# Chunk attention and a swish MLP on one core: the transposition of one more unit goes to the transfers, and list positions move in blocks 1, 2 and 6 to 8

## The chip, the cores and the metric

The kernel runs on one core of a Trainium2 chip. The time is the device time of one execution in microseconds (us); several executions are taken and their median is quoted. The engines are named as the profile names them: PE is TensorE (matmuls), PEld its weight loads, DVE VectorE, ACT ScalarE, POOL GpSimd and SP SyncE. In this kernel POOL and SP issue transfers only, POOL the loads of inputs, SP the stores of outputs and the transposing transfers.

## What is computed

The inputs are q, k and v of 8 batches x 8 heads x 576 positions x 64, and an MLP with `w_in` (512 x 2048), `w_out` (2048 x 512) and a `beta` for each of the 2048 hidden columns.

```python
# attention inside chunks of 64 positions, for every batch and head
scores = scale * np.matmul(q_c, k_c.transpose(0, 1, 2, 4, 3))
attn = softmax(scores)                      # over the 64 keys of the chunk
x = np.matmul(attn, v_c) -> (4608, 512)     # tokens x (heads * 64)
# MLP with swish-beta
h = x @ w_in
g = h * (1.0 / (1.0 + np.exp(-beta * h)))
out = g @ w_out                             # 4608 x 512, float32
```

## The kernel before

**Units and blocks.** Tokens are worked in 18 units of 256 (four chunks, all eight heads) and nine blocks of 512 tokens, so block j holds units 2j and 2j+1. All matmul operands are float16, the sums float32.

**A unit of attention.** `load_qk` and `load_v` bring q, k and v in from POOL's queue. `emit_T` turns q and k around (head dimension onto the partitions). Up to unit XU−1 this is done by two VectorE transposes (L164) out of 256 KB loads (L112); from unit XU on by two transposing transfers on SP's queue (L159), and then each load is made of two halves of 128 KB with another layout (L106). XU is 9 before. After each `emit_T(u)` the loads of units up to u+4 are issued, as far as they have not been; four buffers for q and four for k set when POOL may issue them, three each for the turned tiles. `emit_sc` makes the scores in one of two forms: 64 matmuls of K=32 (L232) up to XU−1, 32 matmuls of K=64 (L219) from XU on; then ACT takes the exponential (L241, L225). `emit_pv` multiplies by v, with a column of constants that gives the denominators (L270; L256 from unit 8). `emit_norm` divides on VectorE, one half of the unit at a time (L307 and L313 up to unit 7; other lines from unit 8, where WV begins). The normalised half x is turned either on PE with a copy on ACT (`emit_xt_pe`, L329, units 0 to 5) or by a transposing transfer on SP (`emit_xt_dma`, L348, issued right after each norm, units 6 on). The result, `xt`, is what the first matmul of the MLP reads.

**The first matmul of the MLP.** `emit_m(j, m)` makes 128 of the 2048 hidden columns of block j: four matmuls of 128x512 into a PSUM tile `hps` (L372), tanh on ACT (L384) and the gate on VectorE (L360), which writes `gt`. From block QB = 6 on only the columns m = 0 to 3 go this way, with a silu on ACT (L381) and a scale `mg` on VectorE (L356). The other three groups of columns (i = 1, 2, 3) are formed by seven products of 256-wide sub-blocks in place of eight: `emit_q(j, i, s)`, in four steps s, into two PSUM tiles `qx` and `qz` (L484), with copies by ACT (L503) and adds by VectorE (L506) into `hq`. `emit_q_silu(j, i, part)` then runs two silus on ACT (L513) for part 2, 1 or 0, each on a quarter of `hq`, and `emit_q_scale` (L527) writes `gt`.

**The second matmul.** It also takes seven products for eight, in the order 1, 2, 6, 5, 7, 3, 4, each in two halves of eight 128x256 matmuls (L585). `emit_wt` (L427) and `emit_sum` (L436) form the sums of `w_out` and of `gt` that some products use, on VectorE. The accumulators of a block are two PSUM tiles, `ya` for products 1, 6, 7, 4 and `yb` for 2, 5, 3 (for block 1 they come from the four `ps_p` buffers and are called `acc`; while those are in use, in block 2, two buffers are left for `hps` and for the other tiles of that pool). An accumulator is read out after products 1, 6, 5 and 4 by an ACT copy (L602) and after 2, 7 and 3 by a VectorE add (L605), and the store goes out on SP (L539).

**What sets the order.** Nothing is reordered by a scheduler: instructions stand on each engine in the order in which the program emits them. For blocks j = 1 to 8 that order is a list. Each item has a position between 0 and about 1 in the block and a priority for equal positions; the list is sorted and emitted (lines 738 to 851). In block j the list holds the first matmul of block j (`m`, or the `LANE` of m and q items), the second matmul of block j−1 (`prod`, `sum`), and attention of the units of later blocks (`sc`, `pv`, `norm`, `T`). Block 2 also has attention of unit 5, and units 6 and 7, which block 3 reads; block 3 has units 8 to 10. `T 8`, `T 9` and `T 10` are in block 2's list. In blocks 6 to 8 a q item with step 2 brings two silu items (parts 2 and 1) and a scale item; their positions come from c, e and f, which are the lane's positions at that item, one item on and two items on.

Of the kernel before, what the change touches and what calls it, by code (L numbers as in the profile page):

```python
# [8 lines left out]
FP32 = mybir.dt.float32  # L9
# [6 lines left out]
def kernel(  # L16
# [16 lines left out]
    KFF = DFF // 128  # L33
# [21 lines left out]
    ps_y, qs_p, osl_p = [], [], []  # L55
# [20 lines left out]

    blocks = [(u, 2) for u in range(0, NU, 2)]
    NB = len(blocks)
    XU = 9
    WV = 8  # L80
    QB = 6
    unit_block = {}
# [15 lines left out]
    def load_qk(u):  # L98
        for src, dst, nm in ((q, q_t, "qu"), (k, k_t, "ku")):
            t = qk_p.tile([128, H, 2, D], FP16, tag=nm, name=nm)  # L100
            if u >= XU:
                dst[u] = t
# [46 lines left out]
    qT = {}  # L149
    kT = {}  # L150

    def emit_T(u, which=("kT", "qT")):
        for nm in which:
# [3 lines left out]
            dst[u] = t  # L157
            if u >= XU:
                nc.sync.dma_start_transpose(  # L159
# [50 lines left out]
    def emit_sc(u, split=False):  # L210
        qt, kt = qT.pop(u), kT.pop(u)
        sc = ps_s[0].tile([128, 2, H, CH], FP32, tag="s", name="sc")
        if u >= XU:
            qx, kx = (t.rearrange("p h s e -> p (h s e)").rearrange("p (j c t) -> p j c t", j=H, c=2)
# [29 lines left out]
    def emit_pv(u, halves=(0, 1)):  # L244
        et = et_t[u]
        if u >= WV:
# [3 lines left out]
            for n in (7, 0, 1, 2, 3, 4, 5, 6):  # L250
                for r in range(2):
# [3 lines left out]
                    for c in range(2):  # L255
                        nc.tensor.matmul(  # L256
                            out=o[64 * c:64 * c + 64],
                            lhsT=(et[64 * r:64 * r + 64, g % 2, 4 * s + 2 * c + g // 2, :] if u >= XU
                                  else et[64 * r:64 * r + 64, s, 4 * c + g, :]),
# [292 lines left out]
    def emit_prod(j, p, t):  # L552
        last = j == NB - 1
        if p == 1 and t == 0:
            if j == 1:
                a = [ps_p[0].tile([128, 512], FP32, tag="p", name="acc") for _ in range(2)]
            else:
                a = [ps_y[0].tile([128, 512], FP32, tag=n, name=n) for n in (("yb", "ya") if last else ("ya", "yb"))]
            if last:
                a = [[ps_p[0].tile([128, 512], FP32, tag="p", name="acc") for _ in range(2)], a]  # L560
            acc_t[j] = a
        g = gt_t[j]
        acc = acc_t[j][0 if p in (1, 6, 7, 4) else 1]
        acc, dst = (acc[t][:, 0:256],) * 2 if last else (acc, acc[:, 256 * t:256 * t + 256])
        c0 = t * 128
        for kk in range(8):
            lhsT = {
                1: lambda: g[:, kk, c0:c0 + 128],
                2: lambda: g[:, 8 + kk, c0:c0 + 128],
                3: lambda: sm[3][:, kk, c0:c0 + 128],  # L570
                4: lambda: g[:, 8 + kk, 256 + c0:256 + c0 + 128],
                5: lambda: sm[0][:, kk, c0:c0 + 128],
                6: lambda: sm[1][:, kk, c0:c0 + 128],
                7: lambda: sm[2][:, kk, c0:c0 + 128],
            }[p]()
            rhs = {
                1: lambda: w_at(0, kk, 0),
                2: lambda: w_at(1, kk, 0),
                3: lambda: w_at(1, kk, 1),
                4: lambda: wt[3][:, kk, :],  # L580
                5: lambda: wt[0][:, kk, :],
                6: lambda: wt[1][:, kk, :],
                7: lambda: wt[2][:, kk, :],
            }[p]()
            nc.tensor.matmul(  # L585
                out=dst,
                lhsT=lhsT,
                rhs=rhs,
                start=(p in (1, 2, 5) and kk == 0 and (t == 0 or last)),
                stop=(kk == 7 and (t == 1 or last)),  # L590
                skip_group_check=True,
            )
        if t == 0 and not last:
            return
        flush_stores()
        r, c, how = {1: (0, 0, "copy"), 2: (0, 0, "add"), 6: (0, 1, "copy"), 5: (1, 1, "copy"),
                     7: (1, 1, "add"), 3: (0, 1, "add"), 4: (1, 0, "copy")}[p]
        key = (j, r, c, t if last else None)
        if how == "copy":
            o = osl_p[0].tile([128, 256], FP32, name="osl") if last else osb_p.tile([128, DM], FP32, tag="osb", name="osb")  # L600
            oq_t[key] = o
            nc.scalar.copy(out=o, in_=acc)  # L602
        else:
            o = oq_t[key]
            nc.vector.tensor_tensor(out=o, in0=acc, in1=o, op=ALU.add)  # L605
        if p in (2, 7, 3, 4):
            late.append(key)
# [6 lines left out]
    with tc.manual_schedule():  # L614
# [104 lines left out]
        def att_items(u, a0, w):  # L719
            it = [(a0, 2, ("sc", u)), (a0 + 0.36 * w, 3, ("pv", u)), (a0 + 0.361 * w, 3, ("norm", u, 0)),  # L720
                  (a0 + (0.42 if u >= WV else 0.50) * w, 3, ("norm", u, 1))]
            if u >= WV:
                it.append((a0 + (0.45 * w if u == 9 else 0.005), 3, ("T", u + 3)))
            return it

        ATT = {2: ((6, 0.36, 0.27), (7, 0.60, 0.27)),
# [11 lines left out]
        for j in range(1, NB):  # L738
# [6 lines left out]
            items = []  # L745
            if j == 1:
                items += [(0.04 * m, 0, ("h", m)) for m in range(8)]
                items += [(0.32 + 0.0850 * (m - 8), 0, ("m", m)) for m in range(8, KFF)]
                items += [(0.30, 3, ("T", 4)), (0.52, 2, ("sc", 4)), (0.70, 2, ("pv", 4)), (0.71, 3, ("norm", 4, 0)),
                          (0.80, 3, ("norm", 4, 1)), (0.56, 3, ("Th", 5, "kT")), (0.63, 3, ("Th", 5, "qT"))]  # L750
                items += [(c, 3, ("wt", i)) for i, c in ((1, 0.47),)]
            else:
                m0 = {2: 0.36, 4: 0.09}.get(j, 0.02)
                if j < QB:
                    items += [(m0 + (1 - m0) * m / KFF, 0, ("m", m)) for m in range(KFF)]
                else:
                    lane = LANE[2 if j == QB else j == NB - 1]
                    cost = [1 if it[0] == "q" and it[2] == 3 else 2 for it in lane]
                    for n, it in enumerate(lane):
                        c, e, f = (0.98 * sum(cost[:n + d]) / sum(cost) for d in (0, 1, 2))  # L760
                        items.append((c, 0, it))
                        if it[0] == "m":
                            items.append((c + 0.04, 3, ("mg", it[1])))
                        elif it[0] == "last":
                            pass
                        elif it[2] == 2:
                            if j == NB - 1 and it[1] == 3:
                                f = e
                            items += [(f - 0.002, 2, ("qs", it[1], 2)), (f - 0.001, 2, ("qs", it[1], 1)),
                                      (f + 0.03, 3, ("qt", it[1], 0))]  # L770
                        elif it[2] == 3:
                            items += [(c + 0.001, 2, ("qs", it[1], 0)), (c + 0.04, 3, ("qt", it[1], 1))]
                    if j == QB:
                        items.append((0.01, 6, ("open",)))
                        items += [(0.011+0.001*n, 6, ("tx", QB, n)) for n in range(4)]
                    if j + 1 < NB:
                        items += [(0.70 + 0.06 * n, 5, ("tx", j + 1, n)) for n in range(4)]
                for i, p in enumerate((1, 2, 6, 5, 7, 3, 4)):
                    for t in range(2):
                        w = 1.06 if j == NB - 1 else 0.98  # L780
                        items.append(((0.002 if j >= QB else 0) + w * (2 * i + t) / 14, 1, ("prod", p, t)))
                if j == NB - 1:
                    for i, c in ((2, 0.72), (0, 0.80), (1, 0.86)):
                        items.append((c, 4, ("pre", i)))
                for i in range(4):
                    s0 = (0.01, 0.08, 0.25, 0.33)[i] if j == 2 else 0.005 + 0.07 * i
                    if j >= QB:
                        s0 = (0.08, 0.15, 0.33, 0.48)[i] if j == QB else (0.003, 0.10, 0.33, 0.48)[i]
                    items.append((s0, 4, ("sum", i)))
                if j == 2:  # L790
                    items += [(c, 3, ("wt", i)) for i, c in ((2, 0.36), (3, 0.55))]
                    items += [(0.03, 0, ("sc", 5)), (0.06, 2, ("xp", 4, 0)), (0.09, 2, ("xp", 4, 1)),
                              (0.17, 2, ("pv", 5)), (0.18, 3, ("norm", 5, 0)), (0.19, 3, ("norm", 5, 1)),
                              (0.24, 3, ("T", 6)), (0.53, 3, ("T", 7)), (0.60, 3, ("T", 8)), (0.61, 3, ("T", 9)), (0.80, 3, ("T", 10)),
                              (0.30, 2, ("xp", 5, 0)), (0.32, 2, ("xp", 5, 1))]
                for jw, i, c, d in ((3, 2, 0.10, 0.22), (4, 1, 0.21, 0.22), (4, 3, 0.10, 0.22)):
                    if jw == j:
                        items += [(c + d * n, 5, ("ws", i, n)) for n in range(4)]
                for u, a0, w in ATT.get(j, ()):
                    items += att_items(u, a0, w)  # L800
# [90 lines left out]
```

## Time and profile before

| Quantity | us |
|---|---|
| Median of three runs | 276.55 |
| Lowest and highest | 276.26, 276.83 |
| The profiled execution's own time | 276.39 |
| Its span in the profile | 274.6 |
| PE busy in the span | 266.6 |
| DVE, ACT, POOL busy | 210.0, 166.8, 95.2 |

The span is the part of the execution that the hardware profiler covers; the execution's own time is 1.8 us longer. PE is busy for 97% of the span, from about 17 us on nearly without a break. The granted TensorE clock of the profile is 1.00 in every stretch asked for. The page also lists how busy the DMA engines are: nines (90% and more) in the first 25 of 40 slices, up to about 172 us, and mostly one to three tenths from about 190 us.

The timeline view gives for each group of instructions its start, the busy time from the first start to the last end, the engine, the line, the operation with its tiles, the form, the count, and in brackets the idle time of that engine before the group with what ended it. Matmuls are pipelined, so neighbouring groups of PE overlap a little. `L372` is line 372 of the kernel printed above.

In these terms block 2 runs from about 63 us to 96.5, block 3 begins at 96.49, the blocks with q groups lie after 183 us, and the last block begins near 233.

### The profile page before, as it was taken

What the parts mean: (1) busy time and instruction counts of PE and PEld (TensorE: products, weight loads), DVE (VectorE), ACT (ScalarE), POOL (GpSimd) and SP (SyncE); (2) the same over time, 40 slices, a digit from 0 to 9 for tenths busy, and PEclk for the clock granted to TensorE, in tenths of its full rate; (3) what the DMA queues carried; (4) which work ended last, traced back from release to release, by engine and by line L of the source; (5) the groups of instructions that cost most, each with busy time, mean ns of one, the idle gap of its engine ahead of it and who ended that gap; (6) DMA issues with size and microseconds to landing.
All of it is one profiled execution on the core that took longest, in us unless ns stands there. A gap on an engine that the chain in (4) does not pass through costs nothing.

```text
span 274.6 us, 7824 instructions
## 1 busy us (share of the span) xinstructions
PE 266.6 (97%) x3237; PEld 184.8 (67%) x3237; DVE 210.0 (76%) x394; ACT 166.8 (61%) x300; POOL 95.2 (35%) x122
## 2 busy tenths in 40 slices
PE   7799999999999999999999999999999999999995
PEld 2575445847665666666666666668887887778874
DVE  3567666899998598678977896759896977777961
ACT  2388416976664565556655655576768495858721
POOL 8954478489639935333445200000000000000000
PEclk9999999999999999999999999999999999999999
DMA  9999999999999999999999999853111102110223
GB/s 137 170 195 203 190 181 187 235 171 172 173 149 168 171 174 153 176 146 146 158 153 195 133 137 197 183 147 80 41 54 60 41 0 79 38 41 1 78 79 115
DMA packets 141763, 36.43 MB, mean 133 GB/s; under 512 B 125856, under 2 KB 141216, under 8 KB 141728
## 3 DMA queue, kind: packets, MB, share of 16 engines
q0 software_dynamic: 99136, 18.10, 83.3%
q1 hardware_dynamic: 42592, 17.84, 35.7%
q8 instruction: 25, 0.41, 0.6%
q14 instruction: 10, 0.08, 0.1%
HBM read 36.71 MB, written 9.44 MB: 168 GB/s over the span
## 4 chain that ended last, share of the span: by engine, by line
PE 78%; DVE 10%; ACT 5%; issue 3%; DMA 2%; POOL 0%; DVEq 0%; ACTq 0%; POOLq 0%
PE hps L372 28%; PE ya L585 14%; PE yb L585 11%; PE ops L397 5%; PE acc L585 5%; PE qx L484 4%; PE qz L484 4%; DVE gt L360 3%; ACT hq L513 3%; DMA sm<-in_k_dram 2%; DVE gt L527 2%; PE sc L232 2%; DVE sm L436 1%; PE sc L219 1%; PE x L270 1%
## 5 line engine op out<-in xcount | busy, mean ns | idle before, releaser
L372 PE MATMUL hps<-xt,win 128*128 128x512 f16 (+1 forms) x488 | 106.5, 355 | 0.5 <-DVE gt L360 0.3
L384 ACT ACTIVATE sg<-hps,bt 128x512 f32<-128x512 f32 (+1 forms) x111 | 69.3, 635 | 35.0 <-PE hps L372 32.6
L360 DVE SCALAR_TENSOR_TENSOR gt<-sg,hps 128x512 f16<-128x512 f32 (+1 forms) x111 | 67.6, 617 | 27.7 <-ACT sg L384 26.8
L372 PEld LDWEIGHTS <-win 128*128 128x128 f16 x488 | 46.2, 98 | 32.1 <-issue 1.0
L585 PEld LDWEIGHTS <-sm 128*128 128x128 f16 x512 | 49.4, 98 | 12.0 <-issue 0.3
L585 PEld LDWEIGHTS <-gt 128*128 128x128 f16 x384 | 36.9, 98 | 10.3 <-DVE gt L527 0.8
L120 POOL DMA_DIRECT2D vbig<-in_v_dram x40 | 34.0, 864 | 24.8 <-DMA ku<-in_k_dram 7.4
L585 PE MATMUL ya<-wt,sm 128*128 128x256 f16 x200 | 25.9, 273 | 0.0
L527 DVE TENSOR_SCALAR gt<-hq,rb 128x512 f16<-128x512 f32 x36 | 16.3, 483 | 8.4 <-ACT hq L513 7.2
L106 POOL DMA_DIRECT2D qu<-in_q_dram x20 | 17.1, 872 | 14.1 <-DVE qT L164 5.8
L106 POOL DMA_DIRECT2D ku<-in_k_dram x20 | 17.1, 880 | 12.2 <-DMA qu<-in_q_dram 7.8
L513 ACT ACTIVATE hq<-hq,bs 128x256 f32<-128x256 f32 (+1 forms) x36 | 19.2, 612 | 1.8 <-DVE hq L506 1.8
L436 DVE TENSOR_TENSOR sm<-gt 128x2048 f16<-128x2048 f16 (+1 forms) x17 | 19.7, 1156 | 0.3
L602 ACT COPY osb<-ya 128x512 f32<-128x512 f32 x18 | 10.6, 589 | 8.6 <-PE ya L585 7.9
L484 PEld LDWEIGHTS <-ws 128*128 128x128 f16 x144 | 14.1, 98 | 2.4 <-issue 0.7
L241 ACT ACTIVATE et<-sc 128x1024 f16<-128x1024 f32 (+1 forms) x10 | 8.3, 852 | 11.4 <-PE sc L232 11.4
L397 PE MATMUL ops<-wout,gt 128*128 128x512 f16 x64 | 14.7, 379 | 0.0
L585 PE MATMUL yb<-wout,gt 128*128 128x256 f16 x104 | 13.9, 273 | 0.3 <-DVE gt L527 0.2
L585 PE MATMUL yb<-wt,sm 128*128 128x256 f16 x104 | 13.5, 273 | 0.1
L503 ACT COPY hq<-qx 128x512 f32<-128x512 f32 x18 | 10.6, 587 | 4.9 <-PE qx L484 4.8
L585 PE MATMUL ya<-wout,gt 128*128 128x256 f16 x104 | 13.5, 273 | 0.0
L585 PE MATMUL yb<-wout,sm 128*128 128x256 f16 x104 | 13.5, 273 | 0.0
(99 smaller groups left out, 355.7 us busy)
## 6 DMA issues: line engine op xcount, KB each, us to landing
out_dram<-osb SPq DMA_DIRECT2D x32, 256.0 KB, 2.8
vbig<-in_v_dram POOLq DMA_DIRECT2D x32, 128.0 KB, 7.5
qu<-in_q_dram POOLq DMA_DIRECT2D x18, 128.0 KB, 12.5
ku<-in_k_dram POOLq DMA_DIRECT2D x18, 128.0 KB, 14.6
win<-in_moe_w_in_dram POOLq DMA_DIRECT2D x8, 256.0 KB, 8.7
wout<-in_moe_w_out_dram POOLq DMA_DIRECT2D x4, 512.0 KB, 13.2
qu<-in_q_dram POOLq DMA_DIRECT2D x5, 256.0 KB, 7.0
ku<-in_k_dram POOLq DMA_DIRECT2D x5, 256.0 KB, 7.1
```

The costliest lines, as they stand in the source:

```text
L106: nc.gpsimd.dma_start(out=tv[off:off + n, sp], in_=src[b, :, s:s + n, :].rearrange("h p d -> p h d"),)
L120: nc.gpsimd.dma_start(out=vbig[off:off + n, i % NV, :, 0:D], in_=v[b, :, s:s + n, :].rearrange("h p d -> p h d"),)
L360: nc.vector.scalar_tensor_tensor(out=gt_t[j][:, m, c0:c0 + n], in0=sg[:, 0:n], scalar=1.0, in1=hps[:, 0:n], op0=ALU.add, op1=ALU.mult,)
L372: nc.tensor.matmul(out=hps[:, 0:n], lhsT=w_in16[m // 2][:, kk, (m % 2) * 128:(m % 2) * 128 + 128], rhs=xr[:, c0 // CH:(c0 + n) // CH, 2 * ...
L384: nc.scalar.activation(out=sg[:, 0:n], in_=hps[:, 0:n], func=ACTF.Tanh, scale=bt[:, m:m + 1])
L397: nc.tensor.matmul(out=ops, lhsT=gt_t[j][:, kk, t * 128:(t + 1) * 128], rhs=w_out16[kk // 4][:, kk % 4, :], start=(kk == 0), stop=(kk == K ...
L436: nc.vector.tensor_tensor(out=sm[i][:, lo:hi, :], in0=a, in1=b, op=op)
L484: nc.tensor.matmul(out=dst[:, s, :], lhsT=lhsT, rhs=rhs, start=(p in (1, 2, 5) and s == 0 and kk == 0), stop=(s == 1 and kk == 1), skip_gr ...
L503: nc.scalar.copy(out=o, in_=z if p == 5 else x)
L513: nc.scalar.activation(out=o, in_=src, func=ACTF.Silu, scale=bs[:, m:m + 1])
L527: nc.vector.tensor_scalar(out=gt_t[j][:, m, :], in0=hq[:, b].rearrange("p c q -> p (c q)"), scalar1=rb[:, m:m + 1], scalar2=None, op0=ALU. ...
L585: nc.tensor.matmul(out=dst, lhsT=lhsT, rhs=rhs, start=(p in (1, 2, 5) and kk == 0 and (t == 0 or last)), stop=(kk == 7 and (t == 1 or last ...
```

## The change

Five edits, all in the setting of the lists and of two choices:

- XU goes from 9 to 8. Unit 8's q and k then take the other load layout, the transposing transfers and the 32-matmul scores.
- The two names of the accumulators swap with each block: odd blocks take (`ya`, `yb`), even ones (`yb`, `ya`). The last block is 8 and keeps (`yb`, `ya`); block 2, 4 and 6 are the ones that differ.
- Block 1: small steps in the positions of m, scores of unit 4 and the second half-transposition of unit 5.
- Block 2: scores of unit 5 from 0.03 to 0.07, behind the second half of product 1; the transposition on PE of unit 4's halves with them; `T 6` from 0.24 to 0.27; the sums 2 and 3 from 0.25 and 0.33 to 0.28 and 0.36; unit 6 begins at 0.38 rather than 0.36, unit 7's items are spread over 0.33 rather than 0.27; `T 8` goes from 0.60 to 0.50 and so in front of `T 7` (0.53).
- Blocks 6 to 8: for q groups 1 and 2 the part-2 silus are placed at e instead of f, one lane item earlier; for group 3 in blocks 6 and 7 also part 1 and the scale, as in block 8 already.

In the order that results, SP's queue has unit 8's two transposing transfers behind the xt transfer of unit 6's first half and ahead of that of its second half, of unit 9's pair and of both halves of unit 7; and on VectorE the gate of m 10 of block 2 stands ahead of the normalisation of unit 7's second half instead of behind it.

```diff
-    XU = 9
+    XU = 8
...
-                a = [... for n in (("yb", "ya") if last else ("ya", "yb"))]
+                a = [... for n in (("ya", "yb") if j % 2 else ("yb", "ya"))]
...
-        ATT = {2: ((6, 0.36, 0.27), (7, 0.60, 0.27)),
+        ATT = {2: ((6, 0.38, 0.27), (7, 0.60, 0.33)),
...
             if j == 1:
-                items += [(0.32 + 0.0850 * (m - 8), 0, ("m", m)) for m in range(8, KFF)]
-                items += [(0.30, 3, ("T", 4)), (0.52, 2, ("sc", 4)), (0.70, 2, ("pv", 4)), (0.71, 3, ("norm", 4, 0)),
-                          (0.80, 3, ("norm", 4, 1)), (0.56, 3, ("Th", 5, "kT")), (0.63, 3, ("Th", 5, "qT"))]
+                items += [(0.32 + 0.0820 * (m - 8), 0, ("m", m)) for m in range(8, KFF)]
+                items += [(0.30, 3, ("T", 4)), (0.49, 2, ("sc", 4)), (0.70, 2, ("pv", 4)), (0.71, 3, ("norm", 4, 0)),
+                          (0.80, 3, ("norm", 4, 1)), (0.56, 3, ("Th", 5, "kT")), (0.61, 3, ("Th", 5, "qT"))]
...
                         elif it[2] == 2:
-                            if j == NB - 1 and it[1] == 3:
+                            if it[1] == 3:
                                 f = e
-                            items += [(f - 0.002, 2, ("qs", it[1], 2)), (f - 0.001, 2, ("qs", it[1], 1)),
+                            items += [(e - 0.002, 2, ("qs", it[1], 2)), (f - 0.001, 2, ("qs", it[1], 1)),
                                       (f + 0.03, 3, ("qt", it[1], 0))]
...
-                    s0 = (0.01, 0.08, 0.25, 0.33)[i] if j == 2 else 0.005 + 0.07 * i
+                    s0 = (0.01, 0.08, 0.28, 0.36)[i] if j == 2 else 0.005 + 0.07 * i
...
                 if j == 2:
-                    items += [(0.03, 0, ("sc", 5)), (0.06, 2, ("xp", 4, 0)), (0.09, 2, ("xp", 4, 1)),
+                    items += [(0.07, 2, ("sc", 5)), (0.08, 2, ("xp", 4, 0)), (0.12, 2, ("xp", 4, 1)),
                               (0.17, 2, ("pv", 5)), (0.18, 3, ("norm", 5, 0)), (0.19, 3, ("norm", 5, 1)),
-                              (0.24, 3, ("T", 6)), (0.53, 3, ("T", 7)), (0.60, 3, ("T", 8)), (0.61, 3, ("T", 9)), (0.80, 3, ("T", 10)),
+                              (0.27, 3, ("T", 6)), (0.53, 3, ("T", 7)), (0.50, 3, ("T", 8)), (0.61, 3, ("T", 9)), (0.80, 3, ("T", 10)),
```

More of the change, by code (lines that the diff above doesn't have):

```diff
@@ L557, in emit_prod @@
             else:
-                a = [ps_y[0].tile([128, 512], FP32, tag=n, name=n) for n in (("yb", "ya") if last else ("ya", "yb"))]
+                a = [ps_y[0].tile([128, 512], FP32, tag=n, name=n) for n in (("ya", "yb") if j % 2 else ("yb", "ya"))]
             if last:
```

## The prediction

> **What bounds the kernel now.** The page's busy shares come first, then the chain that ended last, then TensorE's own timeline, searched for starts later than its usual cadence.
>
> ```profile
> PE 266.6 (97%) x3237; PEld 184.8 (67%) x3237; DVE 210.0 (76%) x394; ACT 166.8 (61%) x300; POOL 95.2 (35%) x122
> ...
> PE 78%; DVE 10%; ACT 5%; issue 3%; DMA 2%; POOL 0%; DVEq 0%; ACTq 0%; POOLq 0%
> ```
>
> PE is busy 266.6 of 274.6 us at full granted clock, so the change can win only PE work that it removes or one of the few gaps left, and it can lose by opening a gap. All stalls of the stretches that it touches, from PE's timeline (start, busy, group, and in brackets the idle time and who ended it):
>
> ```profile
> 64.20 0.71 PE L232 MATMUL sc<-qT,kT 32*64 32x64 f16 x64 [0.26 <-DVE x L313]
> ...
> 89.64 1.02 PE L372 MATMUL hps<-xt,win 128*128 128x512 f16 x4 [0.34 <-DVE gt L360]
> ...
> 95.80 0.71 PE L232 MATMUL sc<-qT,kT 32*64 32x64 f16 x64
> 96.49 0.81 PE L372 MATMUL hps<-xt,win 128*128 128x512 f16 x3
> ...
> 213.74 0.60 PE L484 MATMUL qz<-tx,ws 128*128 128x256 f16 x4 [0.18 <-DVE hq L506]
> ...
> 238.93 0.60 PE L484 MATMUL qz<-tx,ws 128*128 128x256 f16 x4 [0.18 <-DVE hq L506]
> ...
> 260.99 0.68 PE L585 MATMUL yb<-wout,gt 128*128 128x256 f16 x2 [0.22 <-DVE gt L527]
> ```
>
> Matmuls overlap, so I take a stall as the start-to-start time above the usual one (m, four 128x512 matmuls, 0.87 us; a product's half 0.87; a quarter of q 0.44). That makes them larger than the brackets: 0.34 at 64.20, 0.50 at 89.64, 0.34 each at 213.74 and 238.93, 0.39+0.29 = 0.68 at 260.99. Scores of unit 8 begin at 95.80 and block 3 at 96.49.
>
> VectorE decides at 89.64:
>
> ```profile
> 82.70 0.70 DVE L164 STREAM_TRANSPOSE kT<-ku 128x512 f32<-128x512 f32 x1
> 83.32 0.67 DVE L164 STREAM_TRANSPOSE qT<-qu 128x512 f32<-128x512 f32 x1
> ...
> 88.06 0.20 DVE L307 RECIPROCAL rd<-x 128x8 f32<-128x8 f32 x1
> 88.30 0.69 DVE L313 TENSOR_TENSOR x<-x,rd 128x512 f16<-128x512 f32 x1
> 88.91 0.68 DVE L360 SCALAR_TENSOR_TENSOR gt<-sg,hps 128x512 f16<-128x512 f32 x1
> ```
>
> The gate of m 10 (88.91) stands behind the normalisation of unit 7's second half, and m 12 needs its PSUM buffer, since block 2 leaves m only two.
>
> The transfers are read by the DMA issues on SP's timeline and by the lines' issue-to-landing times:
>
> ```profile
> 80.39 1.23 SPq L159 DMA_TRANSPOSE kT<-ku  x1
> 81.72 1.80 SPq L159 DMA_TRANSPOSE qT<-qu  x1
> 86.80 3.41 SPq L348 DMA_TRANSPOSE xt<-x  x2
> ...
> 91.03 1.57 SPq L159 DMA_TRANSPOSE kT<-ku  x1
> ```
>
> The second xt here, unit 7's second half, goes out at 89.02, takes 6.0 us and lands at 95.05, 1.4 us before block 3's first m reads it at 96.49. That is the margin of this change. The kT of unit 9 issued at 80.39 took 4.4 us, that of unit 10 at 91.03 took 8.4.
>
> **The change, part by part.** Sums are against the profiled execution: span 274.6, 276.39 with the 1.8 around it, 0.16 under the median of 276.55.
>
> *Unit 8 by transfer.* Removed from VectorE: two transposes, 82.70 to 83.99, 1.29 us. Scores of unit 8 become 32 matmuls of K=64 instead of 64 of K=32; such a group advances PE by 0.47 where L232's takes 0.74, so 0.27 off PE. POOL issues four 128 KB loads in place of two 256 KB ones: two more issues of about 0.9 us, hidden in POOL's waits of 1.38 us before 71.66 and 4.39 before 81.31. POOL's load of unit 11's k now waits for unit 8's kT to land (it went out at 83.53; the landing I put near 84.5), and unit 12's q for qT. Everything on POOL behind them can slip by one or two us; scores 9 to 17 have 4 to 13 us of margin, so nothing. On SP two 256 KB transposes are added, behind xt of unit 6's first half and ahead of its second half, unit 9's pair and both halves of unit 7.
>
> *Block 1.* The order on every engine is unchanged: nothing, both ends.
>
> *Scores of unit 5 a half product later.* The 0.34 stall goes. But VectorE runs without a gap from 55.8 to about 75.5, and PE's first wait on it afterwards (the transposition of x of unit 5, reading a half that ends at 69.54) comes at the same time: m 3 at 75.55 instead of 75.57. Gain 0; the ends are 0 and 0.34.
>
> *Units 6 and 7 spread wider.* With VectorE's 1.29 us gone, and the gate of m 10 ahead of the normalisation of unit 7's second half, I replay block 2 with the row durations: scores 7 at 81.03, m 9 85.62, m 10 86.49, product 3's second half 87.35, m 11 88.22, m 12 89.09 without a stall, m 15 93.43, scores 8 at 95.25, block 3 at 95.63 instead of 96.49. That is 0.86: 0.50 (m 12) + 0.27 (scores) + 0.09 (part of the stall before scores 7). The cost: the normalisation ends at 89.80 instead of 88.99, so the xt behind it is issued 0.83 later; at an unchanged 6.0 us it lands at 95.88. The queue in front of it has 512 KB more. Bounds for those: nothing (they are issued some 10 us before it), or 0.86 each, the distance of quiet landings (83.90 and 84.76), which gives 97.6, or 3.04 each, the distance between unit 10's kT and qT (99.46 and 102.50), which gives 102.0. I take half of the 0.86 case, landing 96.7, because POOL's loads keep the queues filled but the pair goes out early. Block 3 then starts at 96.7 against 96.49: 0.2 lost instead of 0.86 gained; ends −0.86 and +5.5.
>
> [...]
>
> *ya and yb by parity, blocks 2 to 7.* A block's product 1 no longer takes the buffer whose copy is youngest. PE shows no wait there in blocks 3 to 7: 0, ends 0 and 0.1 a block.
>
> *The silus of q, blocks 6 to 8.* At 213.74 the qz quarter waits for VectorE's add (213.00–213.69), behind mg, sum and the scale at 209.54, which waits for four silus at 207.99:
>
> ```profile
> 206.69 0.69 ACT L381 ACTIVATE sg<-hps,bs 128x512 f32<-128x512 f32 x1 [2.79 <-PE hps L372]
> 207.50 0.59 ACT L602 COPY osb<-ya 128x512 f32<-128x512 f32 x1
> 207.99 2.13 ACT L513 ACTIVATE hq<-hq,bs 128x256 f32<-128x256 f32 x4
> ```
>
> ACT is idle 2.79 us before 206.69. With part of the silus ahead of it, the chain ends early enough: 0.34 off. But m 3's silu now stands behind four silus, so its mg ends about 209.01 where product 1 wants it at 208.93: a new wait of 0.13 with the semaphore's time. Net 0.21 at each of two boundaries, 0.42; ends −0.68 and +0.8 (the 2.13 us of silus taking over once).
>
> *Last block.* The second silu of group 2 moves one lane item up, into an ACT idle of 250.17–251.23; the chain to the scale that ends at 260.99 runs 0.75 to 0.9 earlier, and of the 0.68 about 0.1 stays: 0.55; ends 0 and 0.68.
>
> Sum: +0.2 − 0.42 − 0.55 = −0.77, 276.39 − 0.77 = 275.6.
>
> **Rivals.** 0.2%, about 0.55 us, is what a measurement of this kernel can tell from no change.
>
> 1. *xt lands in time.* If the unit 8 pair costs the later transfers nothing (landing 95.9) the 0.86 is kept nearly whole: −0.6 to −0.86, with the q gains 276.39 − 1.8 = 274.6. For: ten us between issue and issue. Against: 6.0 us of the xt itself, POOL's loads in between.
> 2. *The silus only trade places.* ACT's order is a list; a silu put ahead delays the one behind. If mg of m 3 costs the full 0.34 and the tail's wait moves to its next one (264.43, 0.27), the q gains fall to about 0.1, and with 0.2 lost in block 3 it is 276.3. For: ACT had m 3's silu first and PE's product behind it. Against: the 2.79 us of ACT idle.
> 3. *Slower: xt of unit 7 lands late.* One mechanism: the two 256 KB transposes, ahead of it on SP's queue, push its landing. With 0.97 gained elsewhere the time equals before at a landing of 97.46, and is slower by 0.55 from 98.0. One at 3.04 and one at 0.86 gives 99.8, 276.39 + 3.3 − 0.97 = 278.7; both at 3.04, 280.9. For: unit 10's pair did land so, and the DMA share of the page is nines throughout here. Against: unit 9's pair and the xt around 80 landed 0.5 to 0.9 apart.
> [...]
> 4. *Scores of unit 5 really gain.* 0.34 kept: 275.3, inside the forecast's range.
>
> **How the numbers follow.** Forecast (landing 96 to 97.2, q gains mostly there) 0.47, its own range 275.0 to 276.2; rival 1 0.17; rival 2 0.20; rival 3 0.16. The range 274.6 to 277.2 leaves out the lower half of rival 1's neighbourhood and most of rival 3. Faster: rival 1 and nearly all of the forecast, 0.62; within 0.2%: rival 2 and the forecast's upper edge, 0.22; slower 0.16.
>
> **What would show it.** Right: in block 2 m 12 starts without a wait; scores of unit 8 read as L219 with 32 matmuls; xt of unit 7's second half is issued near 89.8 and lands near 96.7, and m 0 of block 3 has a short wait on it; near 213 and 238 no wait on L506, at most 0.15 on an mg; near 260 the wait on L527 is gone. Wrong: a wait of over a us on that xt, a wait of m 0 on nothing at all, or new waits on L381's silus larger than those removed.

## The result and the profile after

The changed kernel takes 277.80 us (median of 20 executions, 276.84 to 281.34) where the kernel before takes 276.69 (20 executions, 276.26 to 277.81). The ratio is 1.005, 95% interval 1.0033 to 1.0066: about half a per cent slower, 1.1 us by the medians, where a gain of 0.3% was forecast. Ratios leave out the slow executions, those more than 1.5% above the fastest of their kernel (one of the 20 here, one of six in experiment 2, three of 12 in experiment 3), and so differ a little from those of the medians. The profiled execution took 279.46 us with a span of 277.7.

The page's busy shares and chain of the changed kernel:

```profile
PE 266.6 (96%) x3205; PEld 184.8 (67%) x3205; DVE 209.0 (75%) x392; ACT 167.3 (60%) x300; POOL 97.1 (35%) x124
...
PE 79%; DVE 11%; DMA 5%; ACT 2%; issue 1%; POOL 0%; DVEq 0%; POOLq 0%
```

VectorE has lost its 1.0 us, PE is as busy as before although the scores of unit 8 have become cheaper, and DMA's share of the chain has gone from 2% to 5%. That share is not where the time is lost: the added 3% is a load of q before block 2, 8.02 us from 48.02 on. PE's timeline around the start of block 3 shows the place:

```profile
95.50 0.45 PE L219 MATMUL sc<-qT,kT 64*64 64x64 f16 x32
98.36 1.02 PE L372 MATMUL hps<-xt,win 128*128 128x512 f16 x4 [2.42 <-DVE sm L436]
99.22 1.46 PE L585 MATMUL yb<-wout,gt 128*128 128x256 f16 x8
100.47 1.91 PE L372 MATMUL hps<-xt,win 128*128 128x512 f16 x4
```

The scores of unit 8 are half the matmuls and end at 95.95. Then PE waits 2.42 us before m 0 of block 3. The bracket names a sum on VectorE, but that ended at 97.41, a microsecond earlier; what came at 98.27, just ahead of 98.36, is the landing of xt of unit 7's second half. The same view shows a second loss: from about 99.3 to 103 the matmuls take up to twice their time (an m needs 1.91 us instead of 1.02). The windows of the same kernel (length, busy time of PE, PEld, DVE, ACT and POOL, then the granted clock, DMA share and GB/s):

```profile
96.00:98.30 2.30, 0.00 (x0) 0.00 (x0) 1.36 (x2) 1.02 (x1) 2.30 (x4) 1.00 1.60 201
98.30:99.30 1.00, 0.94 (x5) 0.49 (x6) 0.00 (x0) 0.00 (x0) 0.84 (x2) 1.00 1.53 181
99.30:100.50 1.20, 1.20 (x10) 0.89 (x9) 0.36 (x1) 0.69 (x1) 0.38 (x1) 0.66 1.59 158
100.50:102.00 1.50, 1.50 (x5) 0.42 (x3) 1.46 (x2) 0.59 (x1) 0.20 (x1) 0.50 1.62 156
102.00:103.00 1.00, 1.00 (x34) 0.62 (x34) 0.00 (x0) 0.58 (x1) 0.68 (x1) 0.50 1.60 159
```

The granted clock falls to 0.50 a little over a microsecond after PE is back at work (near 99.7, PE at work from 98.36). At these clocks 1.2 x 0.34 + 1.5 x 0.50 + 1.0 x 0.50 = 1.66 us of PE time are lost there. This second loss is not in every execution: the mean clock of the 20 executions is 0.998 to 1.000 in thirteen (median 277.70 us) and 0.986 to 0.994 in seven (median 279.4). The profile is one of the seven, so 1.7 of its 3.1 us against the profile before are not the typical loss. The wait is: m 0 starts 1.87 us later than before (98.36 against 96.49), and 0.66 of that is won back in the q blocks and the tail. Only this one trace was taken, so that the other six lost their clock at the same place is not shown.

SP's timeline says for the most part why the transfer is late:

```profile
77.61 1.29 SPq L348 DMA_TRANSPOSE xt<-x  x1
79.08 1.23 SPq L159 DMA_TRANSPOSE kT<-ku  x1
80.42 3.84 SPq L159 DMA_TRANSPOSE qT<-qu  x1
84.35 1.22 SPq L348 DMA_TRANSPOSE xt<-x  x1
85.74 1.23 SPq L159 DMA_TRANSPOSE kT<-ku  x1
87.07 2.59 SPq L159 DMA_TRANSPOSE qT<-qu  x1
89.76 2.64 SPq L348 DMA_TRANSPOSE xt<-x  x2
```

The two qT issues hold SP for 3.84 and 2.59 us; before, unit 9's qT took 1.80. Unit 7's first half was normalised at 86.96 and goes out at 89.76, the second was normalised at 90.04 and goes out at 91.07. It then takes 7.2 us (6.0 before) and lands at 98.27.

The q blocks and the tail, PE's timeline after:

```profile
212.02 1.14 PE L585 MATMUL yb<-wout,gt 128*128 128x256 f16 x8
213.00 0.60 PE L484 MATMUL qx<-xt,win 128*128 128x256 f16 x4
...
262.81 1.56 PE L585 MATMUL yb<-wout,gt 128*128 128x256 f16 x8
264.21 1.04 PE L585 MATMUL ya<-wout,gt 128*128 128x256 f16 x8
```

The waits of 0.34 at 213.74 and 238.93 are gone; in the group at 212.02 (1.14 instead of the usual 1.04) one matmul starts 0.09 late. In the tail the group at 262.81 still has 0.52 of the 0.68.

### The profile page after: what moved, and what is told of

Its sections match the earlier page's. It is cut to its first block, busy times and chain, and to the rows that moved or that the text cites. A ratio compares the mean times of both kernels' runs of the same rounds, so it can differ in the third digit from the quotient of the medians.

```text
span 277.7 us, 7764 instructions
## 1 busy us (share of the span) xinstructions
PE 266.6 (96%) x3205; PEld 184.8 (67%) x3205; DVE 209.0 (75%) x392; ACT 167.3 (60%) x300; POOL 97.1 (35%) x124
## 3 DMA queue, kind: packets, MB, share of 16 engines
q1 hardware_dynamic: 44704, 18.37, 36.3%
## 4 chain that ended last, share of the span: by engine, by line
PE 79%; DVE 11%; DMA 5%; ACT 2%; issue 1%; POOL 0%; DVEq 0%; POOLq 0%
PE hps L372 29%; PE ya L585 14%; PE yb L585 13%; PE qx L484 5%; PE ops L397 5%; PE qz L484 4%; PE acc L585 4%; DVE sm L436 3%; DMA qu<-in_q_dram 3%; DVE gt L360 3%; DMA sm<-in_k_dram 2%; DVE x L313 1%; PE sc L219 1%; PE sc L232 1%; DVE gt L527 1%
## 5 line engine op out<-in xcount | busy, mean ns | idle before, releaser
L585 PEld LDWEIGHTS <-gt 128*128 128x128 f16 x384 | 36.9, 98 | 10.7 <-DVE gt L527 0.6
L106 POOL DMA_DIRECT2D ku<-in_k_dram x22 | 18.8, 874 | 18.0 <-DMA qu<-in_q_dram 9.9
L106 POOL DMA_DIRECT2D qu<-in_q_dram x22 | 18.8, 871 | 13.5 <-DMA vbig<-in_v_dram 5.9
L513 ACT ACTIVATE hq<-hq,bs 128x256 f32<-128x256 f32 (+1 forms) x36 | 19.9, 609 | 5.5 <-DVE hq L506 5.5
L585 PE MATMUL yb<-wt,sm 128*128 128x256 f16 x152 | 19.7, 273 | 0.1
L585 PE MATMUL ya<-wt,sm 128*128 128x256 f16 x152 | 19.7, 273 | 0.0
L506 DVE TENSOR_TENSOR hq<-qz,hq 128x512 f32<-128x512 f32 x18 | 12.3, 684 | 1.1 <-ACT hq L503 0.8
L241 ACT ACTIVATE et<-sc 128x1024 f16<-128x1024 f32 (+1 forms) x9 | 7.3, 833 | 9.5 <-PE sc L232 9.4
L278 DVE TENSOR_TENSOR x<-x,rx 128x512 f16<-128x512 f32 (+1 forms) x20 | 11.9, 620 | 0.3
```

The costliest lines, as they stand in the source:

```text
L106: nc.gpsimd.dma_start(out=tv[off:off + n, sp], in_=src[b, :, s:s + n, :].rearrange("h p d -> p h d"),)
L506: nc.vector.tensor_tensor(out=o, in0=x if p == 7 else z, in1=o, op=ALU.add)
L513: nc.scalar.activation(out=o, in_=src, func=ACTF.Silu, scale=bs[:, m:m + 1])
L585: nc.tensor.matmul(out=dst, lhsT=lhsT, rhs=rhs, start=(p in (1, 2, 5) and kk == 0 and (t == 0 or last)), stop=(kk == 7 and (t == 1 or last ...
```

## The experiments

Theory at the outset: the two added transfers hold SP's queue, unit 7's xt goes out late, and everything else in the change gains. Rivals: the later normalisation of unit 7 is to blame (the spread); or it is the amount of transfers that counts, wherever they stand; or the finer loads. Experiments 1 to 4, 5 to 8 and 9 to 12 ran on three different chips, each time with the kernel before beside them; its medians there were 277.00, 276.82 and 276.91 us, and ratios and gains are to these.

**1. Unit 8 back on VectorE, all else as changed.**

```diff
-    XU = 8
+    XU = 9
...
-(0.50, 3, ("T", 8))
+(0.60, 3, ("T", 8))
```

> The changed kernel with unit 8 back on VectorE, two transposes at their old position, all other edits kept. Theory (SP's issuing): the two added transposing transfers hold SP for 5 us, so xt of unit 7 goes out 2 us late and lands after block 3 wants it. Without them the second xt goes out near 89.8 and lands by 96.3, PE waits under 0.5 us there in place of 2.4, no clock dip follows, and the time is 275.6 to 276.3, 0.4 to 1.0 under the kernel before. Rival (the spread): the loss comes from the normalisation of unit 7 that now stands behind the gate of m 10. Then the xt is late here as well, the wait stays above 1 us and the time above 277.

275.70 us (275.06 to 276.16), ratio to the kernel before 0.9953 (0.9935 to 0.9970). Its SP timeline and the start of block 3 on PE:

```profile
80.76 1.23 SPq L159 DMA_TRANSPOSE kT<-ku  x1
82.10 1.75 SPq L159 DMA_TRANSPOSE qT<-qu  x1
87.26 4.28 SPq L348 DMA_TRANSPOSE xt<-x  x2
```
```profile
95.77 0.71 PE L232 MATMUL sc<-qT,kT 32*64 32x64 f16 x64
96.46 1.02 PE L372 MATMUL hps<-xt,win 128*128 128x512 f16 x4
```

The halves of xt leave at 87.26 and 90.34, as they are normalised, the second lands at 95.89, and m 0 follows the scores without a bracket. The normalisation is as late as in the change, so the spread is not the cause. All edits but XU gain 1.3 us together, and XU costs them and more. This kernel is faster than both.

**2. Unit 8's transfers earlier on SP.**

```diff
-(0.50, 3, ("T", 8))
+(0.37, 3, ("T", 8))
```

> The changed kernel with unit 8's transposing transfers placed ahead of both xt transfers of unit 6 (list position 0.37 in place of 0.50), when SP's queue is idle. Theory (SP's issuing): they go out near 72 to 76, the queue is empty when unit 6's xt comes, xt of unit 7 goes out within 0.3 us of its normalisation and lands by 96.5; PE waits under 0.6 us and the time is 275.2 to 276.2. Rival (the number of bytes in transfers, POOL's loads and all, not the place on SP): the landing stays near 98 and the time at 277 to 278. Rival (the spread): as this, above 277.

280.67 us (278.34 to 282.87), ratio 1.0116 (1.0072 to 1.0160). The theory fell, and the time is above the 277 to 278 of the first rival as well, 2.9 us over the changed kernel; the spread is excluded by experiment 1. SP and PE in its profile, which is of the fastest of the six executions (278.34):

```profile
73.06 3.65 SPq L159 DMA_TRANSPOSE qT<-qu  x1
78.10 2.72 SPq L348 DMA_TRANSPOSE xt<-x  x2
80.98 2.96 SPq L159 DMA_TRANSPOSE kT<-ku  x1
84.04 3.97 SPq L159 DMA_TRANSPOSE qT<-qu  x1
88.11 3.65 SPq L348 DMA_TRANSPOSE xt<-x  x2
```
```profile
97.95 1.02 PE L372 MATMUL hps<-xt,win 128*128 128x512 f16 x4 [1.51 <-DVE sm L436]
...
173.80 0.45 PE L219 MATMUL sc<-qT,kT 64*64 64x64 f16 x32 [0.76 <-DMA qT<-qu]
```

Unit 8's pair is out by 77, yet unit 9's pair now takes 2.96 and 3.97 us to issue. The second xt goes out at 90.57, right after its normalisation (90.54), but takes 7.3 us, lands at 97.86, and m 0 starts at 97.95; and 75 us later the scores of unit 16 wait for their qT. So a place ahead of unit 6's xt does not save the time. What makes the other five executions longer, by up to 4.5 us, is not shown by this trace.

**3. Unit 9's transfers behind unit 7's xt.**

```diff
-(0.61, 3, ("T", 9))
+(0.78, 3, ("T", 9))
```

> The changed kernel with unit 9's two transposing transfers moved behind both xt transfers of unit 7; same bytes, same orders on PE, DVE, ACT and POOL. Theory (SP's issuing): SP is free when x of unit 7 is normalised, its halves go out at about 87 and 90, the second lands by 96.8, PE waits about 0.9 us or less; scores of unit 9 have over 4 us of margin and don't wait; time 275.3 to 276.4. Rival (bytes): 277 to 278, landing 98.

278.41 us (276.15 to 282.68, 12 executions), ratio 1.0022 (0.9996 to 1.0048). The ratio is of nine executions; the median of all twelve is 1.4 us over the kernel before, and above the ranges of theory and rival. The local part of the theory came true: in its profile the second xt leaves at 90.04, lands at 95.18, and block 3 does not wait. But the transfers behind are late by what these were spared:

```profile
127.21 1.02 PE L372 MATMUL hps<-xt,win 128*128 128x512 f16 x4 [1.39 <-DMA xt<-x]
...
157.62 1.87 PE L372 MATMUL hps<-xt,win 128*128 128x512 f16 x4 [2.67 <-DMA xt<-x]
...
159.99 1.89 PE L585 MATMUL yb<-wout,gt 128*128 128x256 f16 x8
```

Blocks 4 and 5 wait on their xt, and the granted clock falls to 0.50 during the 2.67, at 157.1. This profile is of the longest execution (282.68), so it shows where such waits arise, not their usual size.

**4. Other PE work ahead of block 3's m 0.**

```diff
-                m0 = {2: 0.36, 4: 0.09}.get(j, 0.02)
+                m0 = {2: 0.36, 3: 0.145, 4: 0.09}.get(j, 0.02)
```

> The changed kernel with m 0 of block 3 moved from position 0.02 to 0.145, behind the second half of product 1, P V of unit 8 and the first half of product 2, so that PE has 2.2 us of other work while the xt transfer is under way; the transfers are as late as in the changed kernel. Theory: the wait of 2.4 us on the transfer shrinks to a few tenths, the granted clock stays at 1.00 after it, and the time is 274.8 to 276.0; the profile shows xt of unit 7 landing as late as 98. Rival: the lateness is passed on to block 3's gates, sums and block 4, and half of it or more comes back later: 276.5 or above.

276.81 us (276.09 to 277.66), ratio 0.9996 (0.9982 to 1.0010): the change's loss is gone, the gain of the first experiment isn't reached. The xt lands at 98.48, as late as in the change, and PE does not notice; the mean clock is 1.000 in ten of its 12 executions and 0.999 in two. What is left is once more a wait for unit 16:

```profile
97.59 0.22 PE L256 MATMUL xe<-vbig,et 64*64 64x65 f16 x4 [0.16 <-ACT et L225]
...
172.34 0.44 PE L219 MATMUL sc<-qT,kT 64*64 64x64 f16 x32 [0.62 <-DMA qT<-qu]
```

The time lies in the rival's range, 0.8 us over the theory's upper end: of the lateness that m 0 was spared, a part came back at 172. It came by way of the loads. SP's issues for unit 16, first in experiment 1 and then here:

```profile
156.70 2.05 SPq L159 DMA_TRANSPOSE kT<-ku  x1
158.86 4.40 SPq L159 DMA_TRANSPOSE qT<-qu  x1
```
```profile
160.53 1.24 SPq L159 DMA_TRANSPOSE kT<-ku  x1
161.87 4.92 SPq L159 DMA_TRANSPOSE qT<-qu  x1
```

Here SP waits 2.8 us for unit 16's k, and qT stands behind kT: it goes out 3.0 us later and lands at 172.21, where the scores start at 172.34. POOL issued that load of k at 147.71 in place of 138.26.

**5. The transposing transfers alone, unread, on top of experiment 1.**

```diff
+(0.50, 3, ("X", 8)),
...
+                elif it[0] == "X":
+                    for n in range(4):
+                        nc.sync.dma_start_transpose(
+                            out=ws[1][n].rearrange("p a b -> p (a b)").rearrange("p (j t) -> p j t", t=128),
+                            in_=(k_t, q_t)[n // 2][8].rearrange("p h r d -> p (h r d)")[:, 512 * (n % 2):512 * (n % 2) + 512],
+                        )
```

> The kernel of the first experiment (unit 8 on VectorE, all other edits of the change) with transposing transfers added that nobody reads: unit 8's q and k, 512 KB in four transfers, at the place on SP's queue where the change has unit 8's own, into a tile that is free until block 4. PE, DVE, ACT and POOL keep their order. Theory (transfer capacity up to about 175 us, of which SP's place is only a part): 1 to 2.5 us slower than the first experiment, 276.7 to 278.2, with waits on xt of unit 7 or on a kT or xt of a later block. Rival (it is the finer loads of unit 8 and POOL's order that cost, not the transposes): 275.4 to 276.2, as the first experiment.

281.43 us (280.76 to 282.61), ratio 1.0166 (1.0140 to 1.0192), 5.7 us over experiment 1 by the medians: more than expected, in the direction of the theory. In its profile the second xt of unit 7 leaves at 93.29 and lands at 100.43:

```profile
95.72 0.71 PE L232 MATMUL sc<-qT,kT 32*64 32x64 f16 x64
100.57 1.86 PE L372 MATMUL hps<-xt,win 128*128 128x512 f16 x4 [4.14 <-DMA xt<-x]
102.23 1.91 PE L585 MATMUL yb<-wout,gt 128*128 128x256 f16 x8
```

The granted clock falls to 0.50 during this wait, at 99.1. Four issues in place of two make SP's part larger than in the change, so the 5.7 is no measure of the change's transfers. It does show that added transposing transfers alone, with the loads in their old form, are enough for a loss of this kind.

**6. The finer loads alone, on top of experiment 1.**

```diff
+                if u == 8:
+                    for r in range(2):
+                        nc.gpsimd.dma_start(
+                            out=t[off // 2:(off + n) // 2, :, r],
+                            in_=src[b, :, s:s + n, :].rearrange("h (p r) d -> p h r d", r=2)[:, :, r],
+                        )
+                    continue
```

> The kernel of the first experiment with unit 8's q and k loaded in runs of 128 bytes instead of 256, four issues for two, same bytes and same layout in the tile; no transfer is added on SP. Theory (transfer capacity, counted in packets): about 2080 more packets, as many as the two transposes add, but taken from POOL's queue early; 0.2 to 1.0 us slower than the first experiment, 275.9 to 276.8. Rival (only SP's queue counts): 275.4 to 276.0.

275.84 us (275.26 to 276.12), ratio 0.9957 (0.9940 to 0.9974), the same as experiment 1. The xt lands at 96.60 and m 0 waits 0.41 by start-to-start time, but the medians are 0.14 apart. The finer loads are not the cause of the loss.

**7, 9 and 10. The q silus, the accumulators' names, and both, each on the kernel before.**

```diff
-                            if j == NB - 1 and it[1] == 3:
+                            if it[1] == 3:
...
-                            items += [(f - 0.002, 2, ("qs", it[1], 2)), ...
+                            items += [(e - 0.002, 2, ("qs", it[1], 2)), ...
```

> The kernel before with the edit on the q silus in blocks 6 to 8 alone. Theory: the waits of 0.34 at two boundaries fall to 0.09, the tail's 0.68 to 0.52, so 0.5 + 0.16 = 0.7 us faster, ratio near 0.9975. Rival (the silus trade places, the mg behind them waits as long): within 0.3 us of before.

```diff
-... for n in (("yb", "ya") if last else ("ya", "yb"))]
+... for n in (("ya", "yb") if j % 2 else ("yb", "ya"))]
```

> The kernel before with the exchange of ya and yb by parity alone. Theory: PE waits for no copy of an accumulator in the kernel before, so nothing changes: ratio 0.999 to 1.001, and the waits of 0.34 on the add of line 506 stay.

Both diffs together:

> The kernel before with the edit on the q silus and the exchange of ya and yb by parity, nothing else. Theory (the two edits are worth something only together): the silus take away the wait of a qz quarter, 0.34 at each of two boundaries, and put in a wait of product 1 of 0.36 on the ACT copy of the accumulator that product 4 has just filled, as the seventh experiment shows; with the other accumulator that wait is gone too, so 0.5 us at the boundaries and 0.16 in the tail, ratio 0.9975, time about 0.7 us under before. Rival: the copy or the mg next to it holds product 1 as long anyway, and the ratio stays within 0.999 to 1.001.

| Kernel | Median, us | Ratio | 95% interval |
|---|---|---|---|
| silus alone | 276.81 | 1.0000 | 0.9985 to 1.0015 |
| names alone | 276.63 | 0.9984 | 0.9964 to 1.0004 |
| both | 276.15 | 0.9978 | 0.9956 to 1.0000 |

With the silus alone the rival of the seventh expectation came true, by another wait than the one it named. PE's timeline of that kernel:

```profile
209.26 1.03 PE L372 MATMUL hps<-xt,win 128*128 128x512 f16 x4
210.49 1.03 PE L585 MATMUL ya<-wout,gt 128*128 128x256 f16 x8 [0.20 <-ACT osb L602]
```

Product 1 waits for the ACT copy of `ya` that product 4 has just filled, 0.36 by start-to-start time, because that copy now stands behind four silus. That is what the wait on the add had cost. With the names alone the waits of 0.34 on line 506 are all still in the profile; the interval includes 1. With both, the same place has no wait above 0.1:

```profile
207.95 1.03 PE L372 MATMUL hps<-xt,win 128*128 128x512 f16 x4
208.81 1.14 PE L585 MATMUL yb<-wout,gt 128*128 128x256 f16 x8
209.78 0.60 PE L484 MATMUL qx<-xt,win 128*128 128x256 f16 x4
```

By the medians the pair gains 0.76 us; its interval just reaches 1, so that the profile's waits carry this reading more than the times do.

**8. Block 2's list alone, on the kernel before.**

```diff
-        ATT = {2: ((6, 0.36, 0.27), (7, 0.60, 0.27)),
+        ATT = {2: ((6, 0.38, 0.27), (7, 0.60, 0.33)),
...
-                    s0 = (0.01, 0.08, 0.25, 0.33)[i] if j == 2 else 0.005 + 0.07 * i
+                    s0 = (0.01, 0.08, 0.28, 0.36)[i] if j == 2 else 0.005 + 0.07 * i
...
-                    items += [(0.03, 0, ("sc", 5)), (0.06, 2, ("xp", 4, 0)), (0.09, 2, ("xp", 4, 1)),
+                    items += [(0.07, 2, ("sc", 5)), (0.08, 2, ("xp", 4, 0)), (0.12, 2, ("xp", 4, 1)),
...
-                              (0.24, 3, ("T", 6)), ...
+                              (0.27, 3, ("T", 6)), ...
```

> The kernel before with block 2's list edits alone (scores of unit 5, units 6 and 7, transposition of unit 6, two sums), unit 8 still on VectorE at its old place. Theory: m 12 does not wait (0.5), xt of unit 7 goes out 0.8 to 1.3 us later than before and lands close to 96, just in time: 0.3 to 0.6 us faster, ratio 0.998. Rival (the later xt eats it all): 0 to 0.4 us slower.

276.33 us, ratio 0.9984 (0.9972 to 0.9997): 0.49 faster, about the 0.50 of m 12, which does not wait in its profile. There xt of unit 7 goes out at 90.36 (89.02 before) and lands at 96.18, in time for m 0 at 96.48. So this later normalisation is harmless as long as nothing is added ahead of its transfer.

**11. Unit 8 by transfer alone, on the kernel before.**

```diff
-    XU = 9
+    XU = 8
```

> The kernel before with XU = 8 alone: unit 8 by transposing transfers at its old list position, behind both xt transfers of unit 6 and ahead of those of unit 7. Theory (transfer capacity and SP's issuing): xt of unit 7 goes out 1 to 3 us later than before and lands near 98, PE waits 1.5 to 3 us at block 3 or as much at a later unit; 1.0 to 3.0 us slower, ratio 1.004 to 1.011. Rival (1.29 us off VectorE and 0.27 off PE outweigh it): faster by 0.3 or more.

279.54 us (278.85 to 281.19), ratio 1.0094 (1.0058 to 1.0131), 2.6 us slower, as the theory had it. SP and PE in its profile:

```profile
84.79 2.12 SPq L159 DMA_TRANSPOSE kT<-ku  x1
87.02 2.61 SPq L159 DMA_TRANSPOSE qT<-qu  x1
89.72 4.07 SPq L348 DMA_TRANSPOSE xt<-x  x2
```
```profile
99.18 1.02 PE L372 MATMUL hps<-xt,win 128*128 128x512 f16 x4 [2.83 <-issue]
```

The second xt leaves at 91.81 (89.02 before) and lands at 99.09. The bracket says "issue", that is, it names no releaser; the landing 0.09 ahead of the start does.

**12. Unit 9 on VectorE too, on top of experiment 1.**

```diff
-    XU = 9
+    XU = 10
```

> The kernel of the first experiment with unit 9 on VectorE as well: 512 KB fewer in transposing transfers, 1.29 us more on VectorE in block 2, scores of unit 9 with 64 matmuls (0.27 more on PE). Theory: no transfer is waited for in the first experiment, so fewer of them win nothing on PE; xt of unit 7 is issued as soon as it is normalised and the margins of later units grow by 1 to 4 us, but the time is 0.3 to 1.0 us above the first experiment, 276.0 to 276.7, from PE and VectorE. Rival (transfers still hold the first experiment back in places): 275.4 or below.

276.68 us, ratio 0.9989 (0.9970 to 1.0008), 1.0 above experiment 1, at the upper end of what the theory said. The two more transposes on VectorE bring a wait in block 2:

```profile
86.92 1.89 PE L372 MATMUL hps<-xt,win 128*128 128x512 f16 x8 [0.67 <-DVE gt L360]
```

So in this kernel one unit more on the transfers costs waits for transfers, and one unit fewer costs waits for VectorE; XU = 9 is between the two.

## Why the prediction was wrong, by its steps

The parts add up: block 2's list 0.9984, silus with names 0.9978, product 0.9962, against 0.9953 for experiment 1, which holds both. Unit 8 by transfer is 1.0094 alone, and 1.005 / 0.9953 = 1.0097 on top of the others.

- *Unit 8 by transfer, its cost on SP: the step that failed.* The prediction added 0.83 us for the later normalisation and "half of the 0.86 case" for the queue: issue at 89.85, landing 96.7. The transfer was issued at 91.07 and landed at 98.27. Of the 1.6 us, 0.2 are a later start of this whole execution (scores of unit 4 are 0.2 late already), 1.0 is SP's issuing (normalised at 90.04, out at 91.07), and 0.4 the flight, 7.2 us where 6.0 and the allowance for the queue came to 6.85. Without the later start, this step makes about 1.5 of the 1.9 us between the 0.77 gained in the forecast and the 1.1 lost. SP's issuing was not in the sum at all: it counted how far landings lie apart, but not how long SP is held while it issues. The rival that ended on the slower side named the pair, its place ahead of the xt and the point from which the kernel is slower (a landing of 98.0), though it too counted landings alone. By its own rule (0.97 gained elsewhere) a landing of 98.27 is 0.8 us slower; with the 0.66 that was gained (0.50 + 0.16) it is 1.1, and the medians are 1.1 apart. It was given a chance of 0.16. The rows for SP's holding were there, 1.80 for unit 9's qT among the lines quoted and, just below them in the profile before, 4.13 for unit 10's:

```profile
92.70 4.13 SPq L159 DMA_TRANSPOSE qT<-qu  x1
```

- *"Scores 9 to 17 have 4 to 13 us of margin, so nothing": failed as well.* Experiments 2 and 4 put a wait on unit 16, experiment 3 on xt of blocks 4 and 5. The slip of POOL's loads that the prediction put at one or two us begins as it said, and then grows. In experiment 4 the loads of k go out 2 us later than in experiment 1 for units 11 and 12, and 8 to 9.5 us later for units 14 to 16. In the profile before, unit 16's qT lands at 167.3, 4.2 us ahead of its scores; that was not enough. Why the slip grows was not separated. The added work falls into a stretch in which the DMA engines are 90% busy or more, up to about 172 us before and 181 after (26 slices of 6.94 us); with the transfers in other places (experiments 2, 3 and 11) a wait stayed, at block 3 or later. Whether SP's holding or the engines' share is the smaller limit of the two stays open: in experiment 2 the second xt is not held by SP at all and loses in flight, in experiment 11 it goes out 2.8 us later than before. In the profile after, the slip begins with POOL's load of unit 11's k, which waits for unit 8's kT:

```profile
86.04 2.25 POOL L106 DMA_DIRECT2D ku<-in_k_dram  x3 [2.26 <-DMA kT<-ku]
```

- *0.27 off PE for unit 8's scores: right* (0.45 busy in place of 0.71).
- *m 12's wait of 0.50: right*, gone in the profile after and 0.49 in experiment 8.
- *Scores of unit 5, gain 0: right in the sum.* The wait moved to the transposition of unit 5's x (69.82, 0.42 by start-to-start time), as forecast. Another 0.17 appeared at 75.78, and the 0.09 hoped for at scores 7 did not come either (0.28 stayed).
- *The q boundaries: the size right, the assignment wrong.* 0.42 was forecast; 0.68 of waits became 0.18, 0.50. But the silus alone are worth nothing, and the exchange of names, which was costed at 0 because PE showed no wait on a copy before, is what lets them count. A wait that a change creates was not looked for in the buffer that the other edit frees.
- *The tail: 0.55 forecast, 0.16 measured.* The scale at the end waits for silus of group 3, which did not move; VectorE is busy without a gap before it, so that the earlier silu of group 2 shortened nothing there.
- *Finer loads hidden: right* in the time (experiment 6). *Block 1: nothing seen.*
- *The loss of clock was in no part of the prediction.* It cost 1.7 us in the profiled execution, and seven of the 20 have a lowered mean clock.

The share of the hardware queue rose from 35.7% of 274.6 to 36.3% of 277.7 us, by 2.8 us for the 512 KB of the two added transfers. That is, as an estimate from these rounded shares, 187 GB/s beside the loads. Experiment 11 moves the same bytes with 36.9% of 277.7 us, 4.4 us more than before, so that the same estimate gives 119 there.

## What to carry to other kernels

In this kernel, with DMA engines that are 90% busy or more up to about 172 us, the transfers moved onto them were paid by readers with a small margin (PE waited 2.42 us in the change, 2.83 in experiment 11), and moving transfers about only chose the reader (1.51 and 0.76 in experiment 2, 1.39 and 2.67 in experiment 3). Compare the gain with that margin (1.4 us here) before counting what the engine is spared. Cost the time for which the issuing engine is held by each transfer (3.84 and 2.59 us for the two qT here), from rows with a backlog, beside the time to landing (7.2 us for the xt), and follow a slip of the loads to the last unit. And look at two edits together when one of them puts work in front of a buffer's release and the other takes away the need for that buffer.

## What was not expected of the hardware

During or after some waits of PE its granted clock fell to 0.50, and the length of the wait did not settle whether it did. In the profiles here it fell with idle times of 2.42, 2.67 and 4.14 us, and stayed at 1.00 with 1.39, 1.51 and, in experiment 11's profile, 2.83. In the start phase of experiment 10's profile it fell after one of 1.52:

```profile
8.18 0.64 PE L200 MATMUL sc<-sm 32*64 32x64 f16 x32 [1.52 <-DVE sm L183]
```

In windows of 0.2 us the half clock lasts 3.4 us in two of these (99.7 to 103.1 after, 8.2 to 11.6 in experiment 10) and 6.8 us in the other two (157.1 to 163.9 in experiment 3, 99.1 to 105.9 in experiment 5). For the work done at half clock that is a price of about 1.7, 3.1 and 2.7 us in the changed kernel and experiments 3 and 5. A lowered mean clock is thus no proof of a late transfer: 2 of 29 executions of the kernel before, beside experiments 9 to 12, have one below 0.995, one of them the longest with 279.74 us. That it is seven of 20 after, and none of 12 in experiment 4, where m 0 does not wait, fits the wait at block 3 as the usual cause. Nearly equal waits, 1.51 in experiment 2 and 1.52 in experiment 10, ended differently, and 2.83 left the clock at 1.00 where 2.42 did not; what decides is not shown.

The issue of a 256 KB transposing transfer is not a fixed cost for SP: in the timelines here it takes from 1.23 us (kT at 79.08 after) to 4.92 (qT at 161.87 in experiment 4). The longer ones were issued with other transfers under way, but so was one of 1.23 (kT at 85.74 after); what decides was not worked out.
